# Gap of 32 words instead of 64 between the two groups of on-chip buffers

## The chip, the core and the metric

The kernel runs on one core of a Trainium2 chip. The metric is the device time of one execution in microseconds (us). The time before is the median of three runs.

## What is computed

The reference is a linear attention without softmax, followed by a two-layer block with softplus. All arrays are float32.

```python
# q, k, v: (8, 8, 576, 64); g_norm: (64,)
kv = np.einsum('bhsd,bhse->bhde', k, v)
o = np.einsum('bhsd,bhde->bhse', q, kv)
rms = np.sqrt(np.mean(o * o, axis=-1, keepdims=True) + 1e-06)
a = o / rms * g_norm
x = a.transpose(0, 2, 1, 3).reshape(4608, 512)
# w_in: (512, 2048); w_out: (2048, 512)
h = x @ w_in
g = np.maximum(h, 0.0) + np.log1p(np.exp(-np.abs(h)))
out = g @ w_out            # (4608, 512)
```

Nearly all the arithmetic is in the two large products, x @ w_in and g @ w_out.

## The kernel before

**Precision.** TensorE's large products take their operands as float32r. Each float32 operand is split into parts (a high part, a low part scaled by 4096, and a combination of both), and three products of parts stand for one float32 product. So each large product in the code has a loop over three parts.

**Stages.** The first stage (up to about 350 us) computes the attention and, for some of the 16 column chunks of w_in and w_out, the two-layer block directly, in blocks of NT = 384 tokens and 64 steps. One step is `mm1` (lines 859 to 865, the matmuls at line 864): twelve matmuls 128x384, with weights from a split chunk of w_in and the split tokens `xv` streamed; and `mm2` (lines 867 to 872, the matmuls at line 871): nine matmuls 128x512, with weights from the split activation `gv` and a split chunk of w_out streamed. Between two of these steps stand small matmuls of the attention (lines 696, 720, 738, 776). The second stage (from about 350 us to the end) does the remaining chunks in 48 wide steps of 512 tokens, two chunks at a time, with seven products instead of eight. Each of the seven, `product` (lines 1059 to 1068, matmuls at line 1066), is six matmuls 128x256 with weights from split forms of w_in and split tokens streamed. Then `mm2` of the wide step (lines 1132 to 1139, matmuls at line 1137) has 24 matmuls 128x512 with weights from `gv` and `g` and a split chunk of w_out streamed. The counts are 64 x 12 = 768 at line 864, 64 x 9 = 576 at line 871, 48 x 7 x 6 = 2016 at line 1066 and 48 x 24 = 1152 at line 1137. Each matmul has a weight load of its own.

**Order.** `Plan` (lines 61 to 203) orders all tasks of all engines before the program is issued, from costs and positions written out in the code. No address enters it. While a product waits for inputs early on, `warm` (line 1232) fills the time with matmuls of the identity by itself. Lines 525 and 526 are sixteen matmuls that help split the first weights, with the identity and its negative as weights.

**Where the buffers lie.** The pools give out on-chip memory in the order of the calls. First come the constants with `ident_r` (line 279) and a small tile `gap0`. Then follows a first group, called A in this text: `units`, `gv0`, `g0`, `gv1`, `g1`, `early` and `turned` (lines 300 to 305). Then comes `gap1` of SHIFT words (line 306), and then a second group, called B: `pieces`, `w12` to `w14`, `half0` to `half2` and `loads` (lines 307 to 311), and behind it the tiles made later (`raw`, `m`, `sq`). Every tile in A and B has a size that is a multiple of 128 words in each partition, 512 bytes, and the weights and the first streamed word of the large forward matmuls start at multiples of 128 words within their tile. So, modulo 512 bytes, everything in A that these matmuls read starts at one place and everything in B at another, and their distance is SHIFT x 4 bytes. With `units` taken as 0, the addresses before are: `ident_r` at 128, A at 0, B at 256. The groups are used so that a large matmul streams from one and takes its weights from the other: lines 864 and 1066 stream from A (`units`, `early`, `turned`) with weights from B; lines 871 and 1137 stream from B with weights from A.

**Order of the streamed words.** `from_the_end` (line 42) reverses the order in which blocks of a streamed operand and of its result are gone through: blocks of 16 and 8 words at line 1066, blocks of 128 at line 1137, single words in the last of the twelve at line 864, and no reversal elsewhere.

Of the kernel before, what the change touches and what calls it, by code (L numbers as in the profile page):

```python
# [206 lines left out]
def kernel(  # L207
# [80 lines left out]
    const.tile([P, 8], F32, name="gap0")  # L288

    PIECE = 3 * d_model  # L290
    SHIFT = 64
    spaces = {}

    def space(name, words, late, dtype=F32):

        if (name, late) not in spaces:
            spaces[name, late] = sb.tile([P, words], dtype, tag=name, name=f"{name}_{int(late)}")
        return spaces[name, late]
# [6 lines left out]
    space("turned", PIECE, False)  # L305
    sb.tile([P, SHIFT], F32, name="gap1")
    pieces = sb.tile([P, 12, PIECE], F32R, name="pieces")
# [960 lines left out]
```

## Time and profile before

| what | value |
|---|---|
| time before, median of 3 runs | 860.03 us (860.0 to 860.41) |
| the profiled execution's own time | 858.61 us |
| its span, from the first to the last instruction | 856.8 us |
| granted TensorE clock | 1.000 |
| instructions | 17075 |
| TensorE, matmuls | 843.8 us busy, 98% of the span, 6464 matmuls |
| VectorE | 704.1 us busy, 82% |
| ScalarE | 520.2 us busy, 61% |
| DMA | 167.07 MB, mean 195 GB/s over the span |

The matmuls' ends are modelled and overlap the next matmul's start, so the duration of one is longer than the time from one start to the next. What a matmul costs in a stream of them is the time from its start to the start of the next; this text calls that its step. It is read from the chain of waits, where a run of matmuls of one line is shown with its length and count, and from the timeline, where the starts of two neighbouring groups are subtracted.

### The profile page before, as it was taken

Reading aid. Unit: us, or ns where it says so; the run is one execution under the profiler, and the core shown is the slowest. Engines: PE = TensorE matmul, PEld = TensorE weight load, DVE = VectorE, ACT = ScalarE, POOL = GpSimd, SP = SyncE. Lnnn points to the kernel's source line nnn. Section 1 sums busy time; section 2 is a strip of 40 time slices with the busy share of each in tenths; the row PEclk is TensorE's granted clock in tenths of the full one; section 3 lists DMA queues with packets and bytes.
Section 4 is the critical chain, followed back from the end, with each engine's and each line's share of the span. In section 5 each row is a group of like instructions: output and inputs, shape, how many; then the busy total and the mean of one; then the engine's idle time right before and its main releaser. Section 6 shows DMA issues by size and latency. Waiting matters only on the chain.

```text
span 856.8 us, 17075 instructions
## 1 busy us (share of the span) xinstructions
PE 843.8 (98%) x6464; PEld 754.7 (88%) x6464; DVE 704.1 (82%) x995; ACT 520.2 (61%) x980; POOL 76.1 (9%) x79
## 2 busy tenths in 40 slices
PE   7899999999999999999999999999999999999998
PEld 5678898999898999998999999998999899999996
DVE  7988898888788889798898788878788766788873
ACT  6866665446344567776667665655868555566654
POOL 0342224111113300000000000000000000000000
PEclk9999999999999999999999999999999999999999
DMA  9998997778784755436645456645354753777864
GB/s 275 301 228 218 264 270 244 178 243 221 215 186 118 194 159 183 143 112 202 211 156 167 160 160 203 197 158 182 124 195 138 234 167 103 241 242 239 250 189 130
DMA packets 239778, 167.07 MB, mean 195 GB/s; under 512 B 106320, under 2 KB 198736, under 8 KB 239696
## 3 DMA queue, kind: packets, MB, share of 16 engines
q1 hardware_dynamic: 239392, 165.86, 65.8%
q8 instruction: 50, 0.82, 0.4%
q14 instruction: 32, 0.26, 0.1%
q10 hardware_dynamic: 304, 0.13, 0.1%
HBM read 112.98 MB, written 52.95 MB: 194 GB/s over the span
## 4 chain that ended last, share of the span: by engine, by line
PE 94%; DVE 2%; ACT 1%; DMA 1%; issue 1%; POOL 1%; SPq 0%; DVEq 0%; ACTq 0%
PE banks L1137 31%; PE banks L1066 28%; PE banks L871 16%; PE banks L864 15%; PE banks L720 2%; PE banks L696 2%; DMA loads<-in_v_dram 1%; DMA raw<-in_moe_w_in_dram 0%; PE banks L738 0%; POOL roots L728 0%; PE banks L1232 0%; DVE half L732 0%; DVE m L464 0%; DVE m L460 0%; DVE units L643 0%
## 5 line engine op out<-in xcount | busy, mean ns | idle before, releaser
L1137 PE MATMUL banks<-pieces,gv 128*128 128x512 f32 x768 | 236.8, 390 | 0.0
L1137 PE MATMUL banks<-pieces,g_False 128*128 128x512 f32 x384 | 149.4, 389 | 0.0
L1137 PEld LDWEIGHTS banks<-pieces,gv 128*128 128x128 f32 x768 | 132.5, 188 | 17.2 <-DVE banks L910 0.2
L864 PE MATMUL banks<-units,pieces 128*128 128x384 f32 x768 | 145.6, 338 | 0.0
L871 PE MATMUL banks<-pieces,gv 128*128 128x512 f32 x576 | 143.3, 393 | 0.0
L864 PEld LDWEIGHTS banks<-units,pieces 128*128 128x128 f32 x768 | 135.5, 188 | 4.5
L871 PEld LDWEIGHTS banks<-pieces,gv 128*128 128x128 f32 x576 | 106.2, 188 | 19.0
L1066 PEld LDWEIGHTS banks<-units,pieces 128*128 128x128 f32 x840 | 111.0, 188 | 6.5 <-ACT banks L1112 0.4
L1066 PE MATMUL banks<-units,pieces 128*128 128x256 f32 x840 | 115.2, 280 | 0.0
L886 ACT ACTIVATE half<-banks 128x384 f32<-128x384 f32 x64 | 31.4, 491 | 95.7 <-PE banks L864 89.8
L1127 DVE TENSOR_TENSOR gv<-g_True,gv 128x1024 fp32r<-128x1024 f32 x47 | 57.5, 1223 | 36.3 <-ACT gv L1124 36.3
L1137 PEld LDWEIGHTS banks<-pieces,g_False 128*128 128x128 f32 x384 | 72.1, 188 | 15.0
L1066 PEld LDWEIGHTS banks<-units,w 128*128 128x128 f32 x504 | 66.7, 188 | 3.7 <-ACT banks L1112 0.2
L1066 PE MATMUL banks<-units,w 128*128 128x256 f32 x504 | 69.6, 280 | 0.0
L728 POOL TENSOR_TENSOR roots<-roots,half 128x8 f32<-128x8 f32 x36 | 61.9, 1720 | 3.0
L1130 DVE SCALAR_TENSOR_TENSOR g_False<-gv 128x1024 fp32r<-128x1024 f32 x47 | 57.6, 1225 | 1.5
L1029 DVE TENSOR_TENSOR units<-loads,units 128x1024 fp32r<-128x1024 f32 x42 | 51.2, 1219 | 6.0 <-ACT units L1026 5.9
L1094 ACT ACTIVATE g_True<-banks 128x256 f32<-128x256 f32 x96 | 36.7, 384 | 30.6 <-PE banks L1066 29.9
L1116 DVE TENSOR_TENSOR g_True<-banks,g_True 128x512 f32<-128x512 f32 x48 | 33.1, 690 | 25.8 <-PE banks L1066 19.8
L931 ACT ACTIVATE m<-banks 128x512 f32<-128x512 f32 x72 | 42.1, 595 | 17.7 <-PE banks L1137 12.5
L1032 DVE SCALAR_TENSOR_TENSOR units<-units 128x1024 fp32r<-128x1024 f32 x42 | 51.4, 1224 | 1.7
L1026 ACT ACTIVATE units<-loads 128x1024 fp32r<-128x1024 f32 x42 | 44.4, 1056 | 12.7 <-PE banks L1066 10.1
(115 smaller groups left out, 1248.5 us busy)
## 6 DMA issues: line engine op xcount, KB each, us to landing
loads<-x SPq DMA_DIRECT2D x180, 128.0 KB, 2.7
part<-m SPq DMA_DIRECT2D x72, 256.0 KB, 2.9
m<-part SPq DMA_DIRECT2D x72, 256.0 KB, 3.5
loads<-form SPq DMA_DIRECT2D x45, 256.0 KB, 3.2
form<-loads SPq DMA_DIRECT2D x36, 256.0 KB, 3.0
raw<-in_moe_w_in_dram SPq DMA_DIRECT2D x16, 512.0 KB, 4.6
loads<-in_k_dram SPq DMA_DIRECT2D x32, 256.0 KB, 4.5
loads<-in_v_dram SPq DMA_DIRECT2D x32, 256.0 KB, 4.6
```

The source lines that it names most:

```text
L728: nc.gpsimd.tensor_tensor(out=r.tile, in0=r.tile, in1=half, op=ALU.pow)
L864: nc.tensor.matmul(from_the_end(hp, w), lhsT=w_in.tile[:, i, kd * P:(kd + 1) * P], rhs=from_the_end(xv.tile[:, i, kd], w), start=(m == 0), ...
L871: nc.tensor.matmul(mine[i].tile, lhsT=gv.tile[:, m, i * P:(i + 1) * P], rhs=w_out.tile[:, m], start=(c == cs[0] and m == 0), stop=(c == cs ...
L931: a = add("ACT", 690 if ph == LAST else 600, lambda: nc.scalar.activation(new(ot, [P, d_model]), bank.tile, func=AF.Copy, scale=scale if p ...
L1026: nc.scalar.activation(part_of(0, F32R), xl.tile if m > 1 else xl.tile[:, 0], func=AF.Copy, scale=DOWN)
L1029: nc.vector.tensor_tensor(out=part_of(1, F32R), in0=xl.tile if m > 1 else xl.tile[:, 0], in1=part_of(0), op=ALU.subtract)
L1032: nc.vector.scalar_tensor_tensor(out=part_of(2, F32R), in0=part_of(1), scalar=-RADIX, in1=part_of(0), op0=ALU.mult, op1=ALU.add)
L1066: nc.tensor.matmul(from_the_end(place(q), (16, 8)[kd]), lhsT=w[:, m, at:at + P], rhs=from_the_end(dst.tile[:, m, v, kd] if u < 6 else dst. ...
L1094: nc.scalar.activation(dst, src, func=AF.Softplus, scale=1.0 + E)
L1127: nc.vector.tensor_tensor(out=gvt(1, F32R), in0=gt(), in1=gvt(0), op=ALU.subtract)
L1130: nc.vector.scalar_tensor_tensor(out=gt(F32R), in0=gvt(1), scalar=-RADIX, in1=gvt(0), op0=ALU.mult, op1=ALU.add)
L1137: nc.tensor.matmul(from_the_end(mine[i].tile, P), lhsT=(gvt(m, F32R) if m < 2 else gt(F32R))[:, c, i * P:(i + 1) * P], rhs=from_the_end(ou ...
```

## The change

One constant is halved. The tile `gap1` is 32 words in each partition instead of 64, so `pieces` and everything allocated behind it lie 128 bytes lower. No instruction is added, removed or moved, and no size other than the gap's changes.

```diff
     PIECE = 3 * d_model
-    SHIFT = 64
+    SHIFT = 32
     spaces = {}
```

The constant is used in one place, `sb.tile([P, SHIFT], F32, name="gap1")` at line 306. With `units` at 0 modulo 512 bytes, B moves from 256 to 128. Before, a streamed operand and the weights that are loaded while it streams lie 256 bytes apart in both directions. After, weights in B lie 128 bytes above an operand streamed from A, and weights in A lie 384 bytes above an operand streamed from B, modulo 512.

## Prediction

> **What bounds the kernel now.** I read the page's busy times and its chain first, then the costliest groups, then the chain in stretches.
>
> ```profile
> PE 843.8 (98%) x6464; PEld 754.7 (88%) x6464; DVE 704.1 (82%) x995; ACT 520.2 (61%) x980; POOL 76.1 (9%) x79
> PE 94%; DVE 2%; ACT 1%; DMA 1%; issue 1%; POOL 1%; SPq 0%; DVEq 0%; ACTq 0%
> L1137 PE MATMUL banks<-pieces,gv 128*128 128x512 f32 x768 | 236.8, 390 | 0.0
> L1137 PE MATMUL banks<-pieces,g_False 128*128 128x512 f32 x384 | 149.4, 389 | 0.0
> L864 PE MATMUL banks<-units,pieces 128*128 128x384 f32 x768 | 145.6, 338 | 0.0
> L871 PE MATMUL banks<-pieces,gv 128*128 128x512 f32 x576 | 143.3, 393 | 0.0
> ```
>
> TensorE is busy 98% of the span and carries 94% of the chain; its large matmuls have no idle time ahead of them. So a nanosecond more per matmul goes straight to the end, and a nanosecond less comes off, until VectorE (82%) becomes the bound, 140 us away.
>
> What a matmul costs is its step, from its start to the next one's. In the chain, runs of one line are a start, a length in us and a count:
>
> ```profile
> 187.36 2.08 PE banks L864 x12
> 189.44 2.04 PE banks L871 x9
> 191.49 2.11 PE banks L864 x12
> ...
> 366.35 0.70 PE banks L1137 x3
> ...
> 374.67 0.68 PE banks L1137 x3
> ...
> 414.78 2.80 PE banks L1066 x24
> ...
> 421.02 2.72 PE banks L1137 x12
> ```
>
> Usual steps are 2.72/12 = 226.7 ns for 512 columns (L871 the same, 2.04/9), 2.08/12 = 173.3 ns for 384, 2.80/24 = 116.7 ns for 256. Times the counts: 1728 x 226.7 + 768 x 173.3 + 2016 x 116.7 ns = 391.7 + 133.1 + 235.2 = 760 us of the 856.8. These four lines are the kernel.
>
> The reader is to see that the same instruction doesn't always take the same step. L864 mostly needs 2.11 and sometimes 2.08 for its twelve; L1137 needed 0.70 for three at 366.35 and 0.68 later. The timeline shows a whole run of the third kind:
>
> ```profile
> 398.59 1.51 PEld L1066 LDWEIGHTS banks<-units,pieces 128*128 128x128 f32 x12
> 398.71 1.60 PE L1066 MATMUL banks<-units,pieces 128*128 128x256 f32 x12
> 400.15 0.63 PE L1137 MATMUL banks<-pieces,gv 128*128 128x512 f32 x2
> ```
>
> From 398.71 to 400.15 are twelve matmuls of 256 columns at 1.44/12 = 120.0 ns, not 116.7, with the same operands' groups and no wait among them. And the first weight load starts at 398.59, 0.12 us ahead of its matmul, which is one step: the weights of a matmul are read while the one before it streams. So TensorE runs in one of several rhythms, a settled one (226.7, 173.3, 116.7) and slower ones. What differs is how the two reads run beside each other, as clock, shapes and groups are the same. The change alters just what those two reads have between them.
>
> **The change part by part.** It adds, removes and moves no instruction, DMA or wait; the plan doesn't look at addresses. Its whole effect is the price of a distance.
>
> *The distances after.* I look for rows at 128 and 384 bytes. The identity lies at 128, so L526, which streams from B (256) while L1232's identity is loaded, is a pair at 384; the last L1232 ahead of L864 at 43.75 us streams the identity while weights at 256 are loaded, a pair at 128.
>
> ```profile
> 35.38 0.39 PE L526 MATMUL banks<-pieces,gv 128*128 128x512 f32 x1
> 35.61 0.62 PE L1232 MATMUL banks<-ident_r 128*128 128x512 f32 x2
> ...
> 43.52 0.77 PEld L864 LDWEIGHTS banks<-units,pieces 128*128 128x128 f32 x4
> ```
>
> L526's step is 35.61 - 35.38 = 0.23. L864's first weights load from 43.52 and its first matmul starts at 43.75, so the step there is 0.23 too. With times rounded to 0.01 us, each is 220 to 240 ns against 226.7 settled: no pair at the new distances costs more than 13 ns extra or saves more than 7. That excludes a doubled step; it doesn't tell a settled rhythm from an unsettled one, and both matmuls come just after a wait.
>
> *Price of an unsettled rhythm, by line.* These rows of this case say what a step costs when it hasn't settled:
> - L1066: 120.0 against 116.7, 3.3 ns x 2016 = 6.7 us.
> - L864: six settled steps are 6 x 173.3 = 1.04 us, so where the twelve take 2.11 us and half are settled, the other half take 1.07, 178 ns each, 4.7 more. All 768: 3.6 us. Some 50 of 64 runs pay 0.03 already, 1.5 us. New: 2.1 us.
> - L1137: 0.70/3 = 233 against 0.68/3 = 226.7, 6.7 ns x 1152 = 7.7 us.
> - L871: 6.7 x 576 = 3.9 us, of which its mean of 393 ns beside L1137's 390 and 389 says that about 3.3 ns are paid already, 1.9 us. New: 2.0 us.
>
> Bounds. Upwards: 13 ns for each of 1728 is 22.5 us; L864's and L1066's nearest bound is the same 13 ns: 10 and 26 us, 58 together, twice what the unsettled 233 ns of L1137 ask for. Downwards: the lines' shortest durations, 387 against a median of 389 ns (L1137), 333 against 334 (L864), 279 against 280 (L1066), allow 2, 1 and 1 ns: 1728 x 2 + 768 + 2016 ns = 6.2 us, and 3.4 us of settling (1.5 and 1.9 above) that could vanish. I take the unsettled rows, since they are long runs of the very lines in question.
>
> *Small terms, at nothing.* L720 streams from A with weights from B too, but at 64 columns its run of 64 takes 1.09 us, 17 ns each, with slices that already lie 0 and 256 bytes apart and no two kinds of run; L738, L776 and L525 are about a hundred matmuls, 10 ns each would be 1 us. VectorE's and ScalarE's operands in B move by 128 bytes: the same two-operand subtraction on 1024 elements takes 1223 ns with both in A (L1127) and 1219 ns with one in B (L1029), so place shows no price, and TensorE's time hides it while their buffers come in time; were 1% of VectorE's 704 us exposed, 7 us. DMAs land in B 128 bytes lower; they have 1% of the chain.
>
> *The sum.* Operand streamed from A (L1066, L864; distance 128): 8.8 us. Streamed from B (L1137, L871; distance 384): 9.7 us. The two distances aren't the same, so one may settle where the other doesn't. One direction lost: 858.61 + 9.25, about 867.9 us; both lost: 858.6 + 18.5 = 877.1. The median of the runs shown is 1.4 above the profiled execution, so 869.3 and 878.5 as a median.
>
> The row that a rule bears on is the pair 116.7 and 120.0 ns, same shape and no wait. The Trainium skill, "TensorE: Matmul & The Clock Gate", section "Step-by-step: what each phase is for", says that TensorE reads weights and streamed operand through two independent ports, so that loading the next weights takes nothing from the running matmul. By that rule the distance is worth nothing and the time stays at 860.0. The trace doesn't decide it: two rhythms agree badly with full independence, but they don't show that addresses choose between them.
>
> **The rivals.** The forecast is that one direction stops settling: 869 us, its own range 865 to 873. For it: several rhythms in the trace; new distances that are unequal. Against it: no long run at either distance.
>
> *Both directions stop settling* (or one far worse): 878.5 us, up to 891 if the excess is some 1.7 times what the unsettled rows show. For it: at distance 256, halfway round 512, the two reads start as far apart as they can, and both directions lose that. Against it: at distance 0 (the last L871 ahead of L864 streams and loads from B) the nine still take 2.04 us.
>
> *Nothing changes*: 860.0 us. For it: that same row at distance 0, and a stream that covers 1024 to 2048 bytes while 512 bytes of weights are read, so that any distance is passed on the way. Against it: 116.7 and 120.0. The rule quoted above gives this result too.
>
> *It settles better* (the other side): the new distance lets L864 and L871 settle at once. The place is the start of each run of twelve or nine; the price is the 1.5 + 1.9 = 3.4 us of settling; it decides as soon as settled steps keep their length. 858.6 - 3.4 = 855.2, as a median 856.6; with the shortest durations everywhere 850. For it: twelve in 2.08 exist beside 2.11. Against it: nothing ties settling to a smaller distance.
>
> *The change doesn't do what it says*: excluded by the sizes, all multiples of 512 bytes in A and B, so the gap alone sets the distance.
>
> **How the numbers follow.** One direction lost 0.34, both lost 0.29, nothing 0.21, better 0.16. The predicted time is that of the first, 869. The range runs from 856.5 (the better case's middle, leaving out about 0.08) to 891 (leaving out about 0.09). A measurement of this kernel tells about 0.2%, 1.7 us, from no change. Faster by more: 0.16; within: 0.20; slower: 0.64 (the first two, and 0.01 of the third).
>
> **What would show it.** In the chain of the changed kernel, runs of L1066 over 24 at 2.88 instead of 2.80 and of L864 over 12 at 2.14 would show direction A lost; runs of L1137 over 12 at 2.80 instead of 2.72 direction B. All four unchanged, with the time unchanged, would show the third case. It is wrong in its root if the large matmuls' steps stay and the time moves all the same, with idle time on TensorE behind VectorE, ScalarE or a DMA; or if a step changes by more than 13 ns.

## The result and the profile after

The changed kernel takes 873.71 us in the median of 4 runs (872.82 to 874.13), beside 860.01 us for the kernel before on the same chip (four runs too). The ratio is 1.0156 with a 95% interval of 1.0142 to 1.0169: 13.7 us slower. The profiled execution has a span of 871.0 us where it had 856.8, at a granted clock of 1.000 as before. The order of the instructions on each engine is the same, and so are the numbers of DMA packets and bytes.

The lines of the page that answer to those shown before:

```profile
PE 857.5 (98%) x6464; PEld 761.0 (87%) x6464; DVE 704.8 (81%) x995; ACT 521.5 (60%) x980; POOL 75.9 (9%) x79
PE 94%; DMA 2%; DVE 1%; ACT 1%; SPq 1%; issue 0%; POOL 0%; DVEq 0%; ACTq 0%
L1137 PE MATMUL banks<-pieces,gv 128*128 128x512 f32 x768 | 240.5, 394 | 0.0
L1137 PE MATMUL banks<-pieces,g_False 128*128 128x512 f32 x384 | 151.4, 394 | 0.0
L864 PE MATMUL banks<-units,pieces 128*128 128x384 f32 x768 | 146.0, 339 | 0.0
L871 PE MATMUL banks<-pieces,gv 128*128 128x512 f32 x576 | 145.8, 397 | 0.0
```

TensorE is still busy 98% of the span and still has 94% of the chain. It has grown by 13.7 us of busy time, VectorE by 0.7 and ScalarE by 1.3. No idle time stands ahead of the large matmuls. So no wait was added there; the matmuls themselves are slower: 394 ns in the mean at line 1137 where they were 390 and 389, 397 at line 871 where they were 393.

The chain of waits after, with start, length and count of each run:

```profile
193.02 2.11 PE banks L864 x12
195.13 2.09 PE banks L871 x9
...
443.81 2.88 PE banks L1066 x24
446.69 2.79 PE banks L1137 x12
```

Read against the rows of before: nine at line 871 took 2.04 us and take 2.09, twenty-four at line 1066 took 2.80 and take 2.88 (2.87 in other turns), twelve at line 1137 took 2.72 and take 2.79. Line 864's twelve took 2.08 or 2.11 and still take 2.11. The slower runs stand in every turn of the wide steps, not in one stretch. Compared matmul by matmul, the changed kernel is 0.5 us behind at 40 us, 3.2 at 350, 6.3 at 500, 10.7 at 700 and 14.2 at the end.

The mean step of each line, from the start of a matmul to the start of the next in the two traces (from 89 us on, where another of the four lines follows), gives the account of the 13.7 us (the last column is worked out from the unrounded means):

| line | streams from, distance after | step before, ns | step after, ns | times | us |
|---|---|---|---|---|---|
| 1066, 256 columns | A, 128 | 116.9 | 119.3 | 2016 | 4.9 |
| 1137, 512 columns | B, 384 | 227.1 | 232.2 | 1152 | 5.9 |
| 871, 512 columns | B, 384 | 230.2 | 234.6 | 576 | 2.5 |
| 864, 384 columns | A, 128 | 175.9 | 176.3 | 768 | 0.4 |

The sum is 13.7 us. The way in which it is lost shows in the single steps of one run of twelve at line 1137 (from 441.70 us before, from 446.69 us after), in ns, from the starts in the traces:

```
before   227 227 226 227 227 226 227 227 226 227 227 226
after    234 225 237 229 238 229 238 229 236 230 238 229
```

Before, the step is settled. After, from its third matmul on, it goes back and forth between some 229 and 238 and doesn't settle at 226.7.

### The profile page after: what moved, and what is told of

Read it like the earlier page. It is cut to its first block, busy times and chain, and to the rows that moved or that the text cites. A ratio compares the mean times of both kernels' runs of the same rounds, so it can differ in the third digit from the quotient of the medians.

```text
span 871.0 us, 17075 instructions
## 1 busy us (share of the span) xinstructions
PE 857.5 (98%) x6464; PEld 761.0 (87%) x6464; DVE 704.8 (81%) x995; ACT 521.5 (60%) x980; POOL 75.9 (9%) x79
## 4 chain that ended last, share of the span: by engine, by line
PE 94%; DMA 2%; DVE 1%; ACT 1%; SPq 1%; issue 0%; POOL 0%; DVEq 0%; ACTq 0%
PE banks L1137 30%; PE banks L1066 28%; PE banks L871 16%; PE banks L864 15%; PE banks L696 2%; PE banks L720 2%; DMA raw<-in_moe_w_in_dram 1%; DMA loads<-in_v_dram 1%; PE banks L738 0%; PE banks L1232 0%; DMA w<-in_q_dram 0%; SPq L766 0%; DVE half L732 0%; PE banks L776 0%; POOL roots L728 0%
## 5 line engine op out<-in xcount | busy, mean ns | idle before, releaser
L1137 PE MATMUL banks<-pieces,gv 128*128 128x512 f32 x768 | 240.5, 394 | 0.0
L1137 PE MATMUL banks<-pieces,g_False 128*128 128x512 f32 x384 | 151.4, 394 | 0.0
L871 PE MATMUL banks<-pieces,gv 128*128 128x512 f32 x576 | 145.8, 397 | 0.0
L1066 PE MATMUL banks<-units,pieces 128*128 128x256 f32 x840 | 117.2, 283 | 0.0
L875 DVE TENSOR_TENSOR gv<-half,gv 128x384 fp32r<-128x384 f32 x64 | 35.4, 554 | 20.9 <-ACT gv L888 20.1
```

Of the source, the lines that this page charges most:

```text
L871: nc.tensor.matmul(mine[i].tile, lhsT=gv.tile[:, m, i * P:(i + 1) * P], rhs=w_out.tile[:, m], start=(c == cs[0] and m == 0), stop=(c == cs ...
L875: nc.vector.tensor_tensor(out=gv.tile[:, 1], in0=g.tile, in1=gv.tile.bitcast(F32)[:, 0], op=ALU.subtract)
L1066: nc.tensor.matmul(from_the_end(place(q), (16, 8)[kd]), lhsT=w[:, m, at:at + P], rhs=from_the_end(dst.tile[:, m, v, kd] if u < 6 else dst. ...
L1137: nc.tensor.matmul(from_the_end(mine[i].tile, P), lhsT=(gvt(m, F32R) if m < 2 else gt(F32R))[:, c, i * P:(i + 1) * P], rhs=from_the_end(ou ...
```

## The experiments

Two theories were set against each other. **A**: the distance between the streamed operand and the weights that are loaded meanwhile sets the rhythm of TensorE. **B**: the place of the second group counts by itself, or what other engines and DMAs do there.

**m1: the matmuls alone, at 16 distances.** No other engine works. The heart of the kernel, with `w(j, d)` a weight tile that starts d words behind the place of the streamed tiles modulo 512 bytes:

```python
for d in DISTANCES:                       # 0, 32, ..., 480 bytes
    for j in range(36):                   # L51
        nc.tensor.matmul(banks[:, 0], lhsT=w(j, d), rhs=x(j, 512), **flags(j))
    for j in range(36):                   # L53
        nc.tensor.matmul(banks[:, 1, :384], lhsT=w(j, d), rhs=x(j, 384), **flags(j))
    for j in range(36):                   # L55
        nc.tensor.matmul(from_the_end(banks[:, 2, :256], (16, 8)[j % 2]), lhsT=w(j, d), rhs=from_the_end(x(j, 256), (16, 8)[j % 2]), **flags(j))
...
```

> This kernel leaves the reference's computation out: it holds nothing but matmuls, each with its own weight load, in runs of 36 with no wait among them, for 16 distances from 0 to 480 bytes between streamed operand and weights and five forms (512 columns; 384; 256 in reversed blocks of 16 and 8; 512 in reversed blocks of 128; 256 forward). No other engine works meanwhile. Theory A (the distance of weights and streamed operand modulo 512 bytes sets the rhythm of TensorE alone): steps differ by distance; at 256 they are 226.7, 173.3 and 116.7 ns as in the kernel before, and at 128 and 384 some 232 to 233 ns for 512 columns, 176 for 384 and 119 to 120 for 256 reversed, as in the changed kernel. Theory B (the address of the second group by itself, or what other engines and DMAs do there, slows TensorE): the steps are the same at all distances, within 1 ns, as nothing else runs.

The chain of that kernel, the first three runs of the distances 0, 128, 256 and 384:

```profile
16.95 8.16 PE banks L51 x36
25.11 6.26 PE banks L53 x36
31.38 4.32 PE banks L55 x36
...
142.81 8.36 PE banks L51 x36
151.18 6.33 PE banks L53 x36
157.51 4.31 PE banks L55 x36
...
269.05 8.22 PE banks L51 x36
277.27 6.26 PE banks L53 x36
283.54 4.32 PE banks L55 x36
...
394.97 8.36 PE banks L51 x36
403.33 6.34 PE banks L53 x36
409.67 4.31 PE banks L55 x36
```

36 matmuls of 512 columns take 8.16 us at 0 (226.7 ns each) and 8.22 at 256, but 8.36 (232.2) at 128 and at 384. With 384 columns it is 6.26 against 6.33 and 6.34. So for 512 and 384 columns the distance of the weights makes a difference with nothing else running: theory B falls for the size of the effect. For 256 columns this kernel shows none, with 4.32 and 4.31 us. Two things weren't expected. The rows at 128 and 384 are alike, and those at 0 and 256: the period is 256 bytes. (The kernel ran once; its eight distances from 256 on repeat the eight from 0 on, run by run, within 0.06 us.) And 256 columns in reversed blocks took 4.32 us, 120 ns, at 0 and 256 too, where the kernel before has 116.7.

**e1, e2, e3: the same distance elsewhere, and the distances exchanged.**

```diff
-    const.tile([P, 8], F32, name="gap0")     # e1, SHIFT = 64
+    const.tile([P, 40], F32, name="gap0")
-    SHIFT = 64
+    SHIFT = 192                              # e2
-    SHIFT = 64
+    SHIFT = 96                               # e3
```

> The kernel before with the small tile gap0 32 words longer, so that both groups lie 128 bytes higher and the distance stays 256. Theory A: 860.0 us within 0.3%, no step changed. Theory B: the second group no longer starts where it did before, so its price comes too: 866 to 880 us. Between: if the place of the first group counts, some of the 13.7 us.

> Gap of 192 words, 768 bytes: the distance modulo 512 is 256 as before, in bytes it is 512 more. Theory A with a period of 512 bytes: 860.0 us within 0.3%. If the period is longer than 512 bytes, or if the gap's own size counts: another time, by up to the 13.7 us of the change.

> Gap of 96 words: the two distances change places, 384 for what streams from the first group (lines 864, 1066) and 128 for what streams from the second (lines 871, 1137). Theory A, and that both distances are equally bad: 871 to 876 us, with steps near 120 ns at line 1066 and 233 ns at line 1137. Theory A, and that one distance is the bad one for each form: 862 to 885 us with other steps than in the changed kernel. Theory B (a place lower than before is the bad one): 860 us.

e1, with both groups 128 bytes higher, took 860.78 us beside 859.38, a ratio of 1.0013 (1.0004 to 1.0023). e2 took 859.18 us, a ratio of 0.9999 (0.9989 to 1.0009). So neither B's place nor the size of the gap is the cause. e1's interval lies a little above 1, but its large matmuls cost what they did before (390, 389 and 393 ns at lines 1137 and 871). Compared matmul by matmul, its profiled execution is 1.8 us behind at 40 us, in the stretch in which TensorE still waits for inputs, and still 1.8 us behind at the end: the steps after that are those of before. e3, with 384 and 128 exchanged, took 873.32 us, 1.0161 (1.014 to 1.0183), as the change did, and its lines have the changed kernel's means:

```profile
L1137 PE MATMUL banks<-pieces,gv 128*128 128x512 f32 x768 | 240.5, 394 | 0.0
L1137 PE MATMUL banks<-pieces,g_False 128*128 128x512 f32 x384 | 151.3, 394 | 0.0
L871 PE MATMUL banks<-pieces,gv 128*128 128x512 f32 x576 | 145.8, 397 | 0.0
L1066 PE MATMUL banks<-units,pieces 128*128 128x256 f32 x840 | 117.2, 283 | 0.0
```

Theory A holds, and 128 and 384 are equally bad.

**e6: distance 0.** `SHIFT = 128`.

> Gap of 128 words: both groups start at the same place modulo 512. Theory A with a period of 256 bytes, as the matmuls alone showed (0 and 256 alike, 128 and 384 alike): 860.0 us within 0.3%. Theory A with a period of 512 bytes, in which 256 is the place farthest from a collision at 0: slower than the change, above 874 us.

It took 859.49 us beside 859.65, a ratio of 1.0000 (0.9991 to 1.0010). Both groups at the same place modulo 512 cost nothing: a period of 256 bytes in the whole kernel too, and no collision at 0.

**e4, e5: half of the change.** Two more gaps put `gv0` to `g1` at a place of their own. The edit of e4; e5 has 32, 96 and SHIFT = 64 in the same places.

```diff
+    sb.tile([P, 96], F32, name="gap2")
     for i in (0, 1):
         space(f"gv{i}", 4 * WIDE, False, F32R)
         space(f"g{i}", 2 * WIDE, False)
+    sb.tile([P, 32], F32, name="gap3")
     space("early", 2 * PIECE, False)
     space("turned", PIECE, False)
...
-    SHIFT = 64
+    SHIFT = 32
```

> The gap of 32 words stays, and gv0, g0, gv1 and g1 move 128 bytes down modulo 512 by two more gaps, so that lines 871 and 1137 (weights in gv and g, streamed operand in pieces) are 256 apart again and only lines 864 and 1066 keep 128. Theory A: lines 871 and 1137 go back to 226.7 ns, lines 864 and 1066 stay at some 176.5 and 119.5; of the change's 13.7 us some 5 are left: 865 us (863 to 867). If the lines disturb each other at the changes from one to the next: more than 1 us off the sum of this run and the next.

> The kernel before with gv0, g0, gv1 and g1 alone moved 128 bytes up modulo 512: lines 864 and 1066 keep 256, lines 871 and 1137 get 384, as in the changed kernel. Theory A: 232 to 233 ns at lines 871 and 1137, the others as before; some 8.5 us of the 13.7: 868.5 us (866.5 to 870.5).

Both forecasts of theory A failed, e4's by far; what came is the case that e4's text names second, that the lines disturb each other. e4 took 871.56 us beside 859.65, 1.0135 (1.0116 to 1.0155); e5 took 870.91, 1.0121 (1.0102 to 1.0140). The halves are 11.9 and 11.3 us, together 23, and the whole is 13.7. By the mean steps of the profiled executions, taken as in the table of the result and with the lines' numbers of before, e4 loses 10.3 us: 5.9 at line 1066, 0.2 at line 864, and 2.7 and 1.5 at lines 1137 and 871, which were to lose nothing. e5 loses 10.8: 6.1 and 2.7 at lines 1137 and 871, and 1.7 and 0.4 at lines 1066 and 864, which were to lose nothing. The rest, 1.5 us in e4 and 2.5 in e5, is there at 40 us. In the chain of e4 (its lines 1068 and 1139 are 1066 and 1137, moved by the two new lines):

```profile
443.30 2.88 PE banks L1068 x24
446.18 2.75 PE banks L1139 x12
448.92 0.72 PE banks L1068 x6
449.64 2.06 PE banks L1139 x9
```

Line 1139's loads inside a run are at 256 again, yet its twelve take 2.75 us, not 2.72, and its nine 2.06, not 2.04. The steps of such a twelve, from the starts in the trace:

```
e4   231 224 231 235 229 232 231 227 226 227 227 226
e5   234 233 231 229 230 232 241 233 230 232 228 233
```

In e4 it settles at 227, but only after seven matmuls, and most runs of line 1139 have three, six or nine. In e5, at 384, it doesn't settle. In e5's chain the runs of 24 at line 1068 take 2.81 us, near the 2.80 of before, and the runs of 512 columns take what they take in the changed kernel:

```profile
445.65 2.81 PE banks L1068 x24
448.46 2.78 PE banks L1139 x12
451.24 0.71 PE banks L1068 x6
```

So a run doesn't depend on its own distance alone. What precedes it, or the one load where the form changes, counts as well: with `gv0` to `g1` moved, the first weights of line 1139 lie 384 or 128 bytes from what line 1068 streams, where they lie at 0 before and in the change.

**m2: finer, and in another order.** The matmuls alone at 0 to 256 bytes in steps of 16, now with 256 columns run behind 512.

> This kernel leaves the reference's computation out: runs of 36 matmuls of four forms (512 columns in reversed blocks of 128, then 256 in reversed blocks of 16 and 8, then 512 forward, then 384) for 17 distances from 0 to 256 bytes in steps of 16. Theory A with a period of 256: the last distance repeats the first; 512 columns settle at 226.7 ns at 0 and 256 alone or near them. Whether 256 columns, now run behind 512 as in the kernel, settle at 116.7 or at 120.0 at distance 0 and 256 is open: 116.7 says that what ran before chooses the rhythm, 120.0 that the kernel's own addresses do.

At distance 0 the chain of m2 shows the 256-column run (its L53) behind 512 columns (L51):

```profile
16.58 8.16 PE banks L51 x36
24.74 4.20 PE banks L53 x36
```

4.20/36 = 116.7 ns, where m1 had 4.32/36 = 120.0 for the same matmuls at the same distance behind 384 columns. Two rhythms can hold for 36 matmuls on end, and what ran before decides which. The mean steps over each run (the 35 inside it), in ns, from the starts in the trace:

| bytes | 512, reversed blocks | 256, reversed blocks | 384 |
|---|---|---|---|
| 0 | 226.7 | 116.6 | 174.1 |
| 32 | 233.1 | 116.6 | 173.8 |
| 64 | 233.2 | 117.7 | 174.7 |
| 96 | 233.9 | 116.8 | 173.6 |
| 128 | 232.4 | 119.8 | 176.0 |
| 160 | 233.4 | 118.3 | 176.7 |
| 192 | 229.0 | 118.7 | 173.3 |
| 224 | 233.2 | 117.2 | 173.4 |
| 240 | 227.4 | 116.6 | 176.5 |
| 256 | 227.9 | 116.7 | 174.1 |

512 columns settle at 0, 240 and 256 alone; 16 has 233.3. At 240 and 256 the mean is a little above 226.7, since the first four and nine steps of the run lie between 224 and 239; from there on 256 repeats 0.

**m3, m4: is the rhythm handed on?** The matmuls alone, in turns of 24 with 256 columns and 12 with 512, as in the wide steps.

```python
for d, e in PAIRS:        # m3; m4: the twelve at 0, their first load at a distance of its own
    for r in range(8):
        for j in range(24):               # L51
            nc.tensor.matmul(from_the_end(banks[:, 2, :256], (16, 8)[j % 2]), lhsT=w(j, d), rhs=from_the_end(x(j, 256), (16, 8)[j % 2]), **flags(j))
        for j in range(12):               # L53; m4: w(j, 0 if j else first)
            nc.tensor.matmul(from_the_end(banks[:, 3], P), lhsT=w(j, e), rhs=from_the_end(x(j, 512), P), **flags(j))
    ...                                   # 36 with 384 columns at 0, then the next pair
```

> This kernel leaves the reference's computation out: only matmuls, in eight turns of 24 with 256 columns in reversed blocks and 12 with 512 columns in reversed blocks of 128, as in the wide steps, for five pairs of distances (of the 256-column runs, of the 512-column runs): 0 and 0; 128 and 0; 0 and 128; 128 and 128; 96 and 0. All streams start at one place, so the weights that are loaded at a change of form have the distance of the form that comes. If the rhythm is handed on from one run to the next: at 128 and 0 the twelve with 512 columns start at 231 to 236 ns and settle at 226.7 only after some eight, 229.3 in the mean, though every weight load in them lies at 0; 2.75 us for twelve and not 2.72. If the extra time of the two half-changes came from the loads at the changes of form alone (which lay 128 or 384 apart there and lie at 0 here): 2.72 us for twelve at 128 and 0.

In the chain of m3, a turn at 128 and 0, and one at 96 and 0:

```profile
84.53 2.87 PE banks L51 x24
87.40 2.73 PE banks L53 x12
...
243.73 2.81 PE banks L51 x24
246.55 2.77 PE banks L53 x12
```

Behind runs at 128 the twelve settle at once (2.73 us, not the 2.75 expected of handing on; what they have above 2.72 is their last step, in which the first weights of the next 24 are loaded at 128). Behind runs at 96 they need 2.77, 230.5 ns in the mean, though the loads lie at 0. So a rhythm is handed on behind some distances and not behind others. For e4, with 128, that alone was not the cause. But the steps of the twelve behind 96 are 233, 233, 236, 224, 231, 236, 228, 232, 231 and then 227: from the fourth on they are e4's from its second, within 1 ns. So e4's way of settling is seen with the matmuls alone as well; what starts it there isn't.

> This kernel leaves the reference's computation out: the same turns of 24 matmuls with 256 columns and 12 with 512, the twelve at distance 0, but the first weight load of the twelve, which runs while the last of the 24 streams, lies at a distance of its own: five cases (distance of the 24, of that one load): 0 and 0; 0 and 384; 0 and 128; 128 and 0; 128 and 384, the last as in the half-change that kept lines 871 and 1137 at 256. If one load at a change of form is enough to put a run off: 2.75 us for twelve in the last case, with first steps of 231 to 236 ns, and more than 2.72 in the second and third; 2.72 to 2.73 in the first and fourth. If it isn't, and something else in the kernel made line 1137 slow there: 2.72 to 2.73 in all five.

In the chain of m4, a turn with all loads at 0, and one with 128 in the 24 and 384 for the one load, as in e4:

```profile
55.30 2.80 PE banks L51 x24
58.10 2.72 PE banks L53 x12
...
247.54 2.88 PE banks L51 x24
250.42 2.74 PE banks L53 x12
```

One load is enough to put a run off, but for less than expected: 2.74 us, first steps of 237 and 233 ns, then 226.7. With 0 in the 24 and the one load at 128 or 384 it is 2.73, with the same 237 and 233 or 236 and 234: some 16 ns a run. With 128 in the 24 and the one load at 0 it is 2.73 too, there by the last step alone. In e4 the first steps are 231, 224, 231, 235 and it takes seven. So a load at the change of form costs time, but m4 doesn't show e4's steps; what makes line 1139 settle so late there stays open. m4 also shows the two rhythms within one execution: with 0 in the 24 and the one load at 384, the first 24 take 2.88 us behind 36 matmuls of 384 columns (at 67.08 us), and the next 24, behind 512 columns, 2.81 (at 72.69 us).

**e7, e8: a version that might beat both.** m1 and m2 showed 96 and 32 to hold 256 and 384 columns at or near their lowest steps, and 0 to be right for 512. The edit is e4's, with 24, 104 and SHIFT = 24 (e7) and 8, 120 and SHIFT = 8 (e8).

> Three gaps put gv0, g0, gv1, g1 and the second group 96 bytes up modulo 512 and leave units, early and turned at 0: weights in the second group lie 96 from what streams from the first (lines 864, 1066), and lines 871 and 1137 keep 0, which the matmuls alone showed to be as good as 256. At 96 the matmuls alone held 116.7 and 173.4 ns from the first to the last of a run, after any form. If a run's rhythm follows from its own distance: line 864 saves its settling, some 1.6 us, and the others stay: 858.4 us, a ratio of 0.998 to 1.000 against the kernel before. If the rhythm is handed on from run to run, as the two half-changes suggest, lines 871 and 1137 settle anew behind lines 864 and 1066: slower, 862 to 870 us.

> The same with 32 bytes instead of 96. The matmuls alone took 116.7 ns for 256 columns in reversed blocks at 32 and 173.8 for 384, of which the first few of a run were slower. If a run's rhythm follows from its own distance: 859.5 us, a ratio of 0.998 to 1.001. If it is handed on: 862 to 870 us, with slow first steps at lines 871 and 1137.

e7 took 862.96 us, 1.0037 (1.0025 to 1.0050), e8 864.10 us, 1.0053 (1.0035 to 1.0071): both slower than the kernel before, as the second case of both texts had it. The groups of e7 (lines moved by two):

```profile
L1139 PE MATMUL banks<-pieces,gv 128*128 128x512 f32 x768 | 238.4, 391 | 0.0
L873 PE MATMUL banks<-pieces,gv 128*128 128x512 f32 x576 | 144.8, 395 | 0.0
L866 PE MATMUL banks<-units,pieces 128*128 128x384 f32 x768 | 144.7, 338 | 0.0
```

Line 866 gained as meant: its mean step fell from 175.9 to 174.6 ns, 1.0 us in all. Lines 873 and 1139, at the good distance of 0, lost more: their steps grew from 230.2 to 232.8 and from 227.1 to 228.9 ns, 3.6 us in all. (Of the 3.7 us by which e7's profiled execution is behind, 1.4 are there at 40 us and 2.3 come from the steps.) Line 1139 has some three steps of 230 to 233 ns at the head of each run, and line 873's nine go on between 224 and 236, as m3 showed behind 96. The best distance for each form taken by itself is not the best layout. Of those timed here, the ones with all distances at 0 or 256 (before, e1, e2 and e6) are the fastest; that there each run takes up the rhythm of the one ahead fits, but wasn't tested apart.

## Why the prediction was right or wrong

The direction and the place of the loss were right: TensorE's large matmuls became slower with no wait added, and nothing hid it. The longer steps come to 13.7 us, as the time does. That the time lies in the range says less, since 856.5 to 891 holds no change as well.

**The forecast's own case was wrong.** The step that failed is "The two distances aren't the same, so one may settle where the other doesn't". The period is 256 bytes, not 512, so 128 and 384 are one distance (m1, and e3 with the two exchanged at 873.32 us), and both directions stopped settling. That was the second case of the prediction, priced at 878.5 us; the measured 873.7 lies between it and the 869 that was put down, and just outside the 865 to 873 of that case. That 869 is so near is luck: it counts one direction where both were lost, at prices that were too high. At their measured steps, the direction streamed from A was worth 5.3 us and the one from B 8.4.

**The terms, line by line.** Line 1066 was priced at 3.3 ns from the run of 120.0: measured 2.4 ns in the mean (some 3 in runs of 24, where 2.88 us was forecast and 2.87 to 2.88 came). That 120.0 stands for an unsettled distance was luck too: m1 and m2 have 120.0 and 116.6 at one distance, 0. Line 1137 was priced at 6.7 ns from two rows of three matmuls, 0.70 and 0.68, whose rounding alone is several ns: measured 5.1. The forecast length of twelve, 2.80 us, came out as 2.79. Line 871 was to lose 3.4 ns beyond what it already paid: measured 4.4. Line 864 was to lose 2.7 ns: measured 0.5, since at 128 its step goes in turns between some 173 and 182 ns and doesn't stay at the worst of them; its runs of twelve took 2.10 to 2.12 us, not the 2.14 named as the sign, apart from five behind small matmuls with 2.31 and more. The sum for both directions, 18.5 us, was too large by 4.8: 1.8 too much at line 1066, 1.8 at line 1137 and 1.7 at line 864, and 0.5 too little at line 871.

**The case of no change** fell. With nothing but matmuls running, 512 columns took 226.7 ns at distance 0 and 232.2 at 128 (m1). The Trainium skill, "TensorE: Matmul & The Clock Gate", section "Step-by-step: what each phase is for", says that loading the next weights takes no read bandwidth from the running matmul; by that the two would be alike. Here the measurement differs, and it decides. The argument against losing both directions, the unharmed row at distance 0, was a right observation with a wrong conclusion: 0 is as good as 256 (e6), and it is the distances between that are bad.

**That it settles better** fell too: of the 126 runs of lines 864 and 871 only 16 are shorter than before, none by more than 17 ns. The bound of 13 ns per matmul from the pairs with the identity held for the means: the largest mean loss of a line is 5.1 ns.

**What the experiments could not settle.** That the distance makes the steps longer is shown by m1, e1, e2, e3 and e6. Why it does, and whether the two reads share a part of the chip, was not tested. Why the half-changes cost almost as much as the whole was followed to the load at the change of form (m4) and to the rhythm left by the run before (m3); neither shows, behind 128, the seven unsettled steps of e4.

## What to carry to other kernels

In a kernel whose TensorE streams with a weight load behind every matmul, the address distance between streamed operand and next weights can be worth a few per cent of a step: here 0 and 256 bytes were good, and at 128 and 384 the steps of 117, 227 and 230 ns grew by 2.4 to 5.1, those of 384 columns (176) by 0.5. Read it from the length of long runs in the chain divided by their count, and look whether the steps settle or alternate. When one distance is changed, keep those at the changes from one form to the next as well, and time the whole kernel: a distance that is best for a form alone made the forms around it slower.

## What the runs showed of the hardware that was not expected

The steps of the matmuls alone repeat every 256 bytes of distance: 8.16 and 8.22 us for 36 matmuls at 0 and 256, 8.36 at 128 and at 384. The same matmul at the same distance can hold two steps, 116.7 or 120.0 ns, for 36 on end, depending on whether 512 or 384 columns ran before (m2 and m1). A run of 512 columns at distance 0 can need nine matmuls to settle behind a form at 96 (m3). And a single weight load at another distance lengthens the step that it runs in and the two behind it (m4: 121, 237 and 233 ns where 117, 227 and 227 are settled).
